# Batch 1's later K and Q rows in the tile buffers, its squares and scalings open to GpSimd, and a new set of priorities

## The chip, the cores and the metric

The kernel runs on one core of one Trainium2 chip. The metric is the device time of one execution in microseconds (us); smaller is better. A core has five engines with a queue each: TensorE (PE, with its weight loads as PEld), VectorE (DVE), ScalarE (ACT), GpSimd (POOL) and SyncE (SP). SP here issues DMAs only, and POOL issues DMAs beside its own arithmetic.

## What is computed

The reference, cut to what matters: cosine attention over 8 batches, 12 heads, 448 tokens and a head size of 64, then a Fourier mix over tokens and channels, a layer norm and a feed-forward part with 768 and 3072 channels.

```python
q_n = q / (np.linalg.norm(q, axis=-1, keepdims=True) + 1e-06)
k_n = k / (np.linalg.norm(k, axis=-1, keepdims=True) + 1e-06)
scores = np.matmul(q_n, k_n.transpose(0, 1, 3, 2)) / tau
attn = softmax(scores)                       # over the last axis
x = np.matmul(attn, v)                       # (8, 448, 768) after joining the heads
mixed = np.real(np.fft.fft(np.fft.fft(x, axis=1), axis=2))
u = x + mixed
un = (u - mean(u)) / np.sqrt(var(u) + 1e-06)
out = u + np.maximum(un @ w_ch1, 0.0) @ w_ch2
```

## The kernel before

The batches go through the same chain one after another, each overlapping its neighbours: load K and Q, normalise their rows, transpose them, multiply Q by K, exponentials, multiply by V, divide, Fourier mix, layer norm, the product with W1, the positive part, the product with W2, store. PE does all products. The feed-forward products (line 1864 with W1, line 2008 with W2) are most of its work; the attention of the following batch is laid between them.

**The order is planned, not written.** Every step is handed to a planner (class `Plan`) as an operation with the engines that may run it, an estimated duration for each, what it reads and writes, and a priority. `schedule` builds one queue for each engine: it takes, for the engine that can start earliest, the ready operation of best priority. Two tables have the last word. `SHIFT` adds a number of its own to the priority of each of 2833 operations. `HOME` pins an operation to one engine where the code would allow several; in the kernel before it has 70 entries. At run time each engine works through its queue strictly in order and waits on semaphores.

**Batches 0 and 1** are normalised by `first_norm` (line 1179), later ones by `norm` (line 1337). `first_norm` works in groups of head pairs: for batch 0 pair 0, pairs 1 and 2, pairs 3 to 5; for batch 1 pairs 0 to 2 and pairs 3 to 5. Each group has a K part, a Q part and a tail part (the last 64 tokens of both). For each part:

- a load from HBM, issued by SP (line 1231);
- a square into a scratch buffer (line 1249), on ACT for batch 1;
- a reduction over the 64 values of a head on DVE (line 1253);
- logarithm, exponential and reciprocal in `norms` (lines 1173 to 1177), once for a group;
- a scaling of each pair's rows, K and Q at line 1276, tails at line 1272, on DVE for batch 1 and on DVE or POOL for batch 0;
- PE transposes (lines 1299 to 1324) and copies out of PSUM (lines 1290 and 1334).

**Buffers.** Raw rows of batch 0 lie in TX, which later holds sums of W2. Raw rows of batch 1 lie in the place of W2 (W2b, chunks 10 to 23), and the squares of its first Q rows in W2b, chunks 7 to 9. So in `build` the loads of W2's later pieces wait for batch 1: two for the reduction of that square, the others for the scalings. W1's and W2's pieces are loaded by POOL's queue (lines 1154 and 1155), at most three under way. Batch 2's rows go to STG, three buffers in turn (line 1365), and their first load waits for an early piece of W2. E0 and E1 hold the exponentials (line 1442) of alternate head pairs.

**The filler.** `fill` puts small matmuls (line 2258) into gaps of PE's queue: up to the first feed-forward product, and from there to 20 us before the planned end.

Other lines that are named below: 1464, 1477 (Q by K), 1495, 1501 (by V), 1739 (the sum u), 1769 (the layer norm's square), 1797 (copy of transposed rows), 1959 (products with W1 in the last two batches), 1979 (what joins them), 2045 (DVE's addition to the output), 1387 and 2034 (POOL's scalings and additions of later batches), 1653 and 2207 (copies in the Fourier mix).

Of the kernel before, what the change touches and what calls it, by code (L numbers as in the profile page):

```python
# [973 lines left out]
class Kern:  # L974
# [204 lines left out]
    def first_norm(self, b):  # L1179
# [47 lines left out]
        for g, a, n, nt, R3, L, ps in parts:  # L1227
# [9 lines left out]
            for i, (nm, buf, names) in enumerate(ps):  # L1237
# [3 lines left out]
                for j0, j1 in ((0, m),) if b or g < 2 else [(j, j + 1) for j in range(m)] if i < 2 else ((0, m),):  # L1241
# [6 lines left out]
                    def square(e, sq=sq, y_=y_):  # L1248
                        return e.activation(sq, y_, ACTF.Square) if e is self.nc.scalar else e.tensor_tensor(sq, y_, y_, AluOp.mult)
# [1069 lines left out]
```

## Time and profile before

| what | value |
|---|---|
| median of three timed runs | 575.24 us (574.73 to 575.6) |
| the profiled execution, its own time | 575.0 us |
| its span, first to last instruction | 573.2 us |
| granted TensorE clock | 1.000 |
| DMA | 62.19 MB, mean 108 GB/s |
| MB read from HBM, written | 51.90, 11.01 |

A row of the profile names a source line, an engine, an operation and the buffers it writes and reads, then a count, busy microseconds and the mean length in ns. Behind the second bar stands the idle time of that engine just before these instructions, and what ended it ("<-DVE SM L1253" means that a DVE instruction of line 1253 that writes SM released it). A row of waits reads: who waited, for whom, microseconds in all, how often, the longest one. A row of the table by stages gives the stretch, its length, busy time and count for each engine, the granted clock and the DMA share and rate. A busy PE is not PE at its peak, because the lengths of matmuls overlap; PE's idle time is the firmer figure.

### The profile page before, as it was taken

To read this page: it belongs to the slowest core of one execution; us is meant where nothing else is said; L and a number is where in the kernel's file an instruction comes from. 1 tells how busy PE (TensorE), PEld (TensorE's weight loads), DVE (VectorE), ACT (ScalarE), POOL (GpSimd) and SP (SyncE) were. 2 spreads that over 40 slices of the span, in tenths; PEclk is the share of its full clock that TensorE was granted. 3 is DMA by queue.
4 is the path that set the end of the run, shared out by engine and by line. 5 is a ranking of instruction groups with operands and counts; after the bars stand their busy time and mean duration, and the time that the engine had idled before them with its cause. 6 is when DMAs were issued, how large, how long until landed. Compare 5 with 4: busy or idle time off the path is not lost.

```text
span 573.2 us, 16025 instructions
## 1 busy us (share of the span) xinstructions
PE 553.7 (97%) x6616; PEld 432.9 (76%) x6616; DVE 434.0 (76%) x923; ACT 392.9 (69%) x734; POOL 224.4 (39%) x332
## 2 busy tenths in 40 slices
PE   3899999999999899999999999999999999999998
PEld 2578887686787687878778688687886876959695
DVE  9889868987469867986789669965679379886353
ACT  7998976576776885578648886686665761948171
POOL 8522414356328542702380736443524003041304
PEclk9999999999999999999999999999999999999999
DMA  9999997976359645963496569461691200132001
GB/s 213 170 241 202 164 195 108 163 173 111 111 82 113 158 88 111 155 145 70 95 157 76 99 138 125 105 140 23 136 87 27 72 2 17 42 48 66 24 34 56
DMA packets 183945, 62.19 MB, mean 108 GB/s; under 512 B 166688, under 2 KB 181664, under 8 KB 183872
## 3 DMA queue, kind: packets, MB, share of 16 engines
q1 hardware_dynamic: 129824, 38.35, 35.2%
q0 software_dynamic: 54048, 22.81, 32.1%
q8 instruction: 52, 0.85, 0.6%
q14 instruction: 21, 0.17, 0.1%
HBM read 51.90 MB, written 11.01 MB: 110 GB/s over the span
## 4 chain that ended last, share of the span: by engine, by line
PE 78%; DVE 8%; ACT 6%; issue 3%; POOL 2%; DMA 2%; SPq 1%; POOLq 0%; DVEq 0%; ACTq 0%
PE PS L1864 28%; PE PS L2008 26%; PE PS L1959 7%; PE PS L1501 5%; PE PS L1464 5%; PE PS L1495 2%; PE PS L1477 1%; DMA TX<-in_q_dram 1%; ACT F L1769 1%; POOL QH L1387 1%; DVE F L1547 1%; POOL OUTB L2034 1%; PE PS L1685 1%; DVE OUTB L2045 1%; DVE X L1521 1%
## 5 line engine op out<-in xcount | busy, mean ns | idle before, releaser
L1864 PE MATMUL PS<-UNT,W1b 128*128 128x256 bf16 (+1 forms) x1728 | 185.4, 264 | 0.3 <-DVE UNT L1797 0.2
L1442 ACT ACTIVATE E<-PS 128x900 bf16<-128x900 f32 (+1 forms) x192 | 148.7, 827 | 30.3 <-PE PS L1464 24.3
L1864 PEld LDWEIGHTS PS<-UNT,W1b 128*128 128x128 bf16 x1728 | 153.4, 98 | 20.1 <-issue 1.9
L2008 PE MATMUL PS<-W2b,HQ 128*128 128x384 bf16 x720 | 124.9, 326 | 0.0
L1387 POOL TENSOR_TENSOR QH<-STG,SM 128x256 bf16<-128x256 f32 x126 | 84.4, 696 | 86.8 <-DVE SM L1177 65.0
L2008 PEld LDWEIGHTS PS<-W2b,HQ 128*128 128x128 bf16 x720 | 68.8, 98 | 43.1 <-issue 0.4
L2034 POOL TENSOR_TENSOR OUTB<-OUTB,U 128x192 f32<-128x192 f32 x72 | 51.6, 737 | 118.2 <-ACT OUTB L2029 115.6
L2008 PE MATMUL PS<-TX,HQ 128*128 128x384 bf16 (+2 forms) x444 | 76.4, 322 | 0.9 <-DVE OUTB L2045 0.5
L1880 ACT ACTIVATE HQ<-PS 128x512 bf16<-128x512 f32 x86 | 51.2, 595 | 28.8 <-PE PS L1864 27.6
L2108 DVE TENSOR_TENSOR HQ<-HQ 128x1536 bf16<-128x1536 bf16 (+1 forms) x73 | 54.1, 744 | 12.2 <-ACT HQ L1880 7.0
L2008 PEld LDWEIGHTS PS<-TX,HQ 128*128 128x128 bf16 x444 | 41.5, 98 | 27.9 <-DVE OUTB L2045 2.4
L1374 ACT ACTIVATE QH<-STG 128x384 f32<-128x384 f32 x84 | 43.1, 519 | 17.6 <-DVE SM L1376 11.6
L1376 DVE TENSOR_REDUCE SM<-QH 128x6 f32<-128x384 f32 x84 | 45.3, 544 | 11.3 <-ACT QH L1374 11.0
L1501 PE MATMUL PS<-VB,E 128*128 128x65 bf16 x1152 | 51.6, 193 | 0.0
L2067 POOL DMA_INDIRECT out_dram<-OUTB,IDX x21 | 23.7, 1127 | 69.2 <-DVE OUTB L2045 43.4
L1501 PEld LDWEIGHTS PS<-VB,E 128*128 128x128 bf16 x1152 | 47.8, 97 | 1.3
L1880 DVE TENSOR_SCALAR HQ<-PS 128x512 bf16<-128x512 f32 x40 | 27.4, 685 | 23.9 <-PE PS L1864 23.8
L1495 PE MATMUL PS<-VZ,E 128*128 128x130 bf16 x192 | 41.6, 219 | 2.0 <-issue 1.9
L1727 DVE SCALAR_TENSOR_TENSOR U<-ACG,X 128x768 bf16<-128x768 f32 (+4 forms) x39 | 39.5, 1023 | 0.9
L2029 ACT ACTIVATE OUTB<-PS 128x384 f32<-128x384 f32 x36 | 17.7, 491 | 32.2 <-PE PS L2008 29.4
L1464 PE MATMUL PS<-QK 64*128 64x225 bf16 (+2 forms) x864 | 39.2, 227 | 0.5 <-ACT QK L1290 0.5
L1464 PEld LDWEIGHTS PS<-QK 64*128 64x128 bf16 x864 | 25.6, 95 | 13.2 <-issue 6.6
(195 smaller groups left out, 784.5 us busy)
## 6 DMA issues: line engine op xcount, KB each, us to landing
STG<-in_q_dram SPq DMA_DIRECT2D x18, 384.0 KB, 3.9
STG<-in_k_dram SPq DMA_DIRECT2D x18, 384.0 KB, 3.9
VB<-in_v_dram POOLq DMA_DIRECT2D x24, 192.0 KB, 6.4
W2b<-in_moe_w_ch_dram POOLq DMA_DIRECT2D x12, 384.0 KB, 7.4
...
W2b<-in_k_dram SPq DMA_DIRECT2D x2, 576.0 KB, 9.1
W2b<-in_q_dram SPq DMA_DIRECT2D x2, 576.0 KB, 15.9
```

Source lines behind the costliest of these rows:

```text
L1374: P.add("act", lambda a, sq=sq, src=buf[:, w * x:w * x + w]: a.activation(sq, src, ACTF.Square), t_act(w), pr, f"sq{i}_{b}", reads=bn, wri ...
L1376: P.add("dve", lambda v, o=SS[:, i, H // ns * x:H // ns * (x + 1)], sq=sq: v.tensor_reduce(o, sq.rearrange("p (h d) -> p h d", d=DH), AX.X ...
L1387: r = v.tensor_tensor(v3(qh)[:, h:h + 4], v3(buf)[:, h:h + 4], RN[:, i, h:h + 4].unsqueeze(2).to_broadcast((128, 4, DH)), AluOp.mult)
L1442: return a.activation(o, self.PS[:, bk:bk + nc_, 0:SQ2], ACTF.Exp, scale=1.0 / self.tau)
L1464: i = pe.matmul(self.PS[:, bk + h, c0:c0 + n], self.KT[r, jj, kt * 128:(kt + 1) * 128], self.QT[r, jj, cols], start=True, stop=True)
L1495: r = pe.matmul(o, st(6), self.VZ[:, j, :], start=not split, stop=(split and i == 0), skip_group_check=True)
L1501: r = pe.matmul(o[:, 65 * h:65 * h + 65], st(2 * kt + h), self.VB[:, kt, 2 * j + h, :], start=(split and i == h == kt == 0), stop=((not sp ...
L1864: r = pe.matmul(self.PS[:, bk, x * n:(x + 1) * n], self.W1b[:, j, ft * 128:(ft + 1) * 128], self.UNT[:, j, cs], start=(j == 0), stop=(j == ...
L1880: return e.activation(o, i, ACTF.Relu) if e is self.nc.scalar else e.tensor_relu(o, i)
L2008: r = pe.matmul(self.PS[:, bk, 0:n], lhs(f), rhs(f), start=(start and f == 0), stop=(stop and f == NF // 2 - 1), skip_group_check=True)
L2034: r = g.tensor_tensor(self.OUTB[:, ob, xs], self.OUTB[:, ob, xs], self.U[:, ut, xs], AluOp.add)
L2108: P.add("dve", lambda v: v.tensor_tensor(cs(o), cs(a), cs(bq), op), 0.16 + 0.3 * len(ks), -0.5, f"{nm}{ks[0]}_{b}", reads=rd, writes=[x fo ...
```

## The change

In words:

- Batch 1's raw rows of the first group, and the K rows of the second, land in TX; the Q rows and tails of the second land in STG's second and third buffers. Their loads wait for the readers of batch 0's rows that lie there (`told`).
- The squares of batch 1's first Q rows go to E1 instead of W2b. W2's loads no longer wait for batch 1.
- Batch 2's loads into these two STG buffers wait for batch 1's rows in them.
- Squares and scalings of batch 1 may also run on POOL (as may batch 0's squares outside the first group), a square there in pieces of 192 columns.
- The second filler ends 12 us after the first feed-forward product.
- `SHIFT` has a new number for each of its 2833 operations. `HOME` has 206 entries. For the squares and scalings: all of batch 0 are pinned as they were or to ACT and DVE, the first of the K squares of pairs 3 to 5 newly to ACT; of batch 1 all are pinned (squares to ACT, scalings to DVE) but the square of the second K rows and four scalings (K of pair 1, tails of pairs 1, 2 and 5).

The diff without the two tables:

```diff
-PIECE = {"sinp": 1.1, r"sc[KQ]\d_0": 0.95, r"scT\d_0": 0.42, ...
+PIECE = {"sinp": 1.1, r"sc[KQ]\d_[01]": 0.95, r"sq[KQT]\d_[01]": 0.54, r"scT\d_[01]": 0.42, ...
...
-            hf = flat(self.W2b[:, 10:24, :]).bitcast(F32)
-            sw = flat(self.W2b[:, 7:10, :]).bitcast(F32)
+            hf = self.tf[:, 1536:9216].bitcast(F32)
+            sf = flat(self.STG[:])
+            sw = self.E[1][:, 0:2304].bitcast(F32)
...
-            sqn = [[o0, ["SQW"], ["OUT1b", "OUT1d"]], [o0, o0, ["OUT1b", "OUT1d"]]]
+            sqn = [[o0, ["SQW"] + [f"E1_{c}" for c in range(7)], ["OUT1b", "OUT1d"]], [o0, o0, ["OUT1b", "OUT1d"]]]
...
-            K, Q, R = [hf[:, o + x + y * ja:o + x + y * (ja + n)] for x, y in ((0, 384), (1152, 384), (2304, 128))]
+            K, Q, R = [(sf[:, DM + x - 1152 + y * ja:DM + x - 1152 + y * (ja + n)] if b and g and x else hf[:, o + x + y * ja:o + x + y * (ja + n)])
+                       for x, y in ((0, 384), (1152, 384), (2304, 128))]
...
+            told = {}
+            if b:
+                told = {"k": ["Sk1_0", "Sq0_0", "Sq1_0"], "q": ["Sq1_0", "St0_0", "Sk2_0"], "t": ["Sk2_0"]} if g == 0 else {"k": ["Sk2_0", "Sq2_0"]}
...
-                                        dma=(f"lh{g}{nm}{b}", 16 * len(dm)), serve=sv, after=gate, order=self.loads[-1:] if b == 0 else ()))
+                                        dma=(f"lh{g}{nm}{b}", 16 * len(dm)), serve=sv, after=gate + [r for x in told.get(nm, ()) for r in P.rd[x]], order=self.loads[-1:] if b == 0 else ()))
...
-                    es = ("act",) if b else (("act", "dve"), ("act", "dve"), ("act", "dve", "pool"))[g]
+                    es = ("act", "dve") if b == g == 0 else ("act", "dve", "pool")
...
-                        return e.activation(sq, y_, ACTF.Square) if e is self.nc.scalar else e.tensor_tensor(sq, y_, y_, AluOp.mult)
+                        if e is self.nc.scalar:
+                            return e.activation(sq, y_, ACTF.Square)
+                        k = 192 if e is self.nc.gpsimd else w
+                        for x in range(0, w, k):
+                            xs = slice(x, min(x + k, w))
+                            r = e.tensor_tensor(sq[:, xs], y_[:, xs], y_[:, xs], AluOp.mult)
+                        return r
...
-                    sc.append(P.add("dve" if b else ("dve", "pool"), fn, ...
+                    sc.append(P.add(("dve", "pool"), fn, ...
...
-                ... f"ld_{kind}{t}_{b}", writes=bn,
+                ... f"ld_{kind}{t}_{b}", writes=bn + ({1: ["Sq1_1"], 2: ["Sq1_1", "St1_1"]}.get(s, []) if b == 2 else []),
...
-                for c in (3, 4):
-                    self.w[12 + c].deps.add(self.sqw)
-                for c in range(5, 12):
-                    self.w[12 + c].deps.update(self.raw1[3] + (self.raw1[4] if c > 7 else []))
...
-        self.P.fill(first, self.est - 20.0, self.id_op, warm(self.W1b[:, 0, 0:128]), 0.75)
+        self.P.fill(first, first + 12.0, self.id_op, warm(self.W1b[:, 0, 0:128]), 0.75)
```

`sums`, which later overwrites TX with sums of W2, waits in addition for batch 1's rows in TX.

More of the change, by code (lines that the diff above doesn't have):

```diff
@@ L82 @@
 SHIFT = {
-    "iota": {0: -4743.9411}, "iotak": {0: -3749.0012}, "cst": {0: 2295.738}, "iotad": {0: 1504.4864}, "rown": {0: 3564.9514},
-    "tqd": {0: 5876.6502, 1: 5614.4443}, "trd": {0: 5875.7288}, "tpd": {0: -1558.5233, 1: 550.4848}, "tad": {0: 4737.392},
-    "tqs": {0: 4545.6213, 1: 5636.9779}, "trs": {0: 4448.6198}, "tps": {0: -162.6304, 1: -1607.3824}, "tas": {0: -178.9521}, "ktd0": {0: 1975.3204},
[4 rows of a table removed]
-    "mask": {0: 35657.0228}, "sinp": {0: 48649.0823}, "half": {0: 440.6683, 1: 3500.6271}, "sinn": {0: 17464.9799}, "ldt": {0: 44319.0778},
[510 rows of a table removed]
+    "iota": {0: 1055.999}, "iotak": {0: 412.7235}, "cst": {0: 2977.9783}, "iotad": {0: 3978.0742}, "rown": {0: 1060.8053},
@@ L601 @@
+    "tqd": {0: 3803.646, 1: -2997.4266}, "trd": {0: 2432.3949}, "tpd": {0: -2992.3091, 1: -8184.413}, "tad": {0: 15630.733},
+    "tqs": {0: -3148.9211, 1: -3159.9506}, "trs": {0: -2641.2921}, "tps": {0: -3159.405, 1: -3160.3855}, "tas": {0: 5801.7804}, "ktd0": {0: 1123.7336},
[4 rows of a table added]
+    "mask": {0: 44111.9307}, "sinp": {0: 59268.5429}, "half": {0: 3949.4502, 1: 10817.8207}, "sinn": {0: 56970.1711}, "ldt": {0: 45259.1831},
[507 rows of a table added]
 }
 HOME = {
-    "tqd": {0: "dve", 1: "dve"}, "trd": {0: "dve"}, "tas": {0: "act"}, "sinp": {0: "dve"}, "half": {0: "pool", 1: "act"}, "sqK0_0": {0: "act"},
@@ L613 @@
-    "ek1_1": {0: "act"}, "ek2_1": {0: "dve"}, "eq2_1": {0: "act"}, "relu0_0": {0: "act"}, "relu4_0": {0: "act"}, "relu8_0": {0: "dve"},
-    "relu12_0": {0: "act"}, "relu16_0": {0: "act"}
+    "tqd": {0: "dve", 1: "dve"}, "trd": {0: "dve"}, "tad": {0: "act"}, "tas": {0: "act"}, "sinp": {0: "dve"}, "half": {0: "pool", 1: "act"},
+    "sqK0_0": {0: "act"}, "sqQ0_0": {0: "act"}, "sqT0_0": {0: "dve"}, "scK0_0": {0: "dve"}, "scQ0_0": {0: "dve"}, "scT0_0": {0: "dve"},
+    "ek0_0": {0: "act"}, "eq0_0": {0: "act"}, "et0_0": {0: "dve", 1: "act"}, "sqK1_0": {0: "dve"}, "sqQ1_0": {0: "act"}, "scK1_0": {0: "dve"},
@@ new lines @@
+    "scQ1_0": {0: "dve"}, "scT1_0": {0: "dve"}, "scK2_0": {0: "dve"}, "scQ2_0": {0: "dve"}, "scT2_0": {0: "dve"}, "ek1_0": {0: "dve"},
+    "eq1_0": {0: "act"}, "eq2_0": {0: "act"}, "et1_0": {0: "dve", 1: "act"}, "sqK2_0": {0: "act", 1: "act", 2: "dve"},
+    "sqQ2_0": {0: "act", 1: "act", 2: "act"}, "sqT2_0": {0: "act"}, "scK3_0": {0: "dve"}, "scQ3_0": {0: "pool"}, "scT3_0": {0: "dve"},
+    "scK4_0": {0: "pool"}, "scQ4_0": {0: "dve"}, "scT4_0": {0: "dve"}, "scK5_0": {0: "pool"}, "scQ5_0": {0: "pool"}, "scT5_0": {0: "pool"},
@@ new lines @@
+    "ek3_0": {0: "dve"}, "eq3_0": {0: "act"}, "eq4_0": {0: "dve"}, "ek5_0": {0: "act"}, "eq5_0": {0: "dve"}, "et2_0": {0: "dve", 1: "dve"},
+    "gc2_0": {0: "dve"}, "cd0": {0: "dve"}, "cd1": {0: "act"}, "cd2": {0: "dve"}, "cd3": {0: "act"}, "cd4": {0: "act"}, "cd5": {0: "dve"},
+    "halfd": {0: "act"}, "eu00_0": {0: "act"}, "eu01_0": {0: "dve"}, "eu10_0": {0: "dve"}, "eu11_0": {0: "dve"}, "eu20_0": {0: "act"},
[5 rows of a table added]
+    "gc1_1": {0: "act"}, "te0_1": {0: "dve"}, "relu0_0": {0: "act"}, "relu4_0": {0: "act", 1: "dve"}, "relu8_0": {0: "dve"}, "relu12_0": {0: "act"},
@@ new lines @@
+    "relu16_0": {0: "act"}, "relu20_0": {0: "dve", 1: "dve"}, "relu2_0": {0: "dve"}, "relu10_0": {0: "dve"}, "relu18_0": {0: "dve"},
+    "relu22_0": {0: "dve"}, "te1_2": {0: "act"}, "relu16_1": {0: "act", 1: "dve"}, "relu6_1": {0: "act"}, "relu18_1": {0: "act", 1: "dve"},
+    "relu20_1": {0: "act"}, "relu2_1": {1: "dve"}, "relu14_1": {1: "dve"}, "ct0": {0: "dve"}, "ct2": {0: "dve"}, "ct3": {0: "dve"},
+    "te1_3": {0: "act"}, "relu2_2": {0: "act"}, "relu16_2": {0: "dve", 1: "act"}, "relu6_2": {0: "dve"}, "relu8_2": {0: "dve", 1: "act"},
@@ new lines @@
+    "relu22_2": {0: "dve"}, "relu0_2": {1: "act"}, "relu12_2": {1: "act"}, "relu4_2": {1: "act"}, "ktd4": {1: "act"}, "gc1_4": {0: "act"},
+    "z_4": {0: "act"}, "relu2_3": {0: "act"}, "relu14_3": {0: "act", 1: "act"}, "relu16_3": {0: "dve"}, "relu6_3": {0: "act", 1: "act"},
+    "relu18_3": {0: "dve"}, "relu22_3": {0: "act"}, "relu0_3": {1: "act"}, "relu12_3": {1: "dve"}, "relu4_3": {1: "act"}, "relu8_3": {1: "act"},
+    "relu20_3": {1: "act"}, "relu10_3": {1: "act"}, "ktd5": {0: "dve", 1: "dve"}, "gc1_5": {0: "act"}, "z_5": {0: "act"}, "te0_5": {0: "act"},
@@ new lines @@
+    "relu0_4": {0: "act"}, "relu2_4": {0: "act"}, "relu16_4": {0: "act"}, "relu6_4": {0: "act"}, "relu18_4": {0: "act"}, "relu20_4": {0: "act"},
+    "relu22_4": {0: "dve"}, "te0_6": {0: "act"}, "te1_6": {0: "act"}, "relu0_5": {0: "act"}, "relu14_5": {0: "act", 1: "act"},
+    "relu18_5": {0: "act", 1: "act"}, "relu8_5": {0: "dve"}, "relu22_5": {0: "dve", 1: "act"}, "relu12_5": {1: "act"}, "te0_7": {0: "act"},
+    "relu2_6": {0: "dve"}, "relu14_6": {0: "act"}, "relu6_6": {0: "dve"}, "relu8_6": {0: "act"}, "relu20_6": {0: "dve"}, "relu22_6": {0: "act"},
@@ L615 @@
+    "c1r1_6": {0: "dve", 1: "dve"}, "c2r1_6": {0: "act", 2: "dve", 3: "act"}, "c3r1_6": {0: "dve", 1: "act"},
+    "c41_6": {0: "dve", 1: "act", 2: "act", 3: "act"}, "c1r0_7": {0: "dve", 2: "act"}, "c2r0_7": {0: "act", 2: "act"},
+    "c3r0_7": {0: "dve", 1: "dve", 2: "act"}, "c40_7": {1: "dve"}, "c1r2_7": {1: "dve", 2: "dve"}, "c2r2_7": {1: "act"},
+    "c3r2_7": {0: "dve", 1: "dve"}, "c42_7": {1: "act"}
 }
 LATE = {r"W[12]w?_\d+": 1.5, "tmd": 2.0, r"sq\d_\d": 1.5, r"sq[KQT]\d_1": 1.5, r"ktd\d": 2.0, r"qdup\d": 2.0, r"qk\d._[2-7]": 1.5, r"pv\d\d_[2-7]": 1.5, r"pv\d\d_1": 1.0, r"h\d+_[1-7]": 0.5}
-PIECE = {"sinp": 1.1, r"sc[KQ]\d_0": 0.95, r"scT\d_0": 0.42, r"sc\d_\d": 0.6, r"f[avm]\dp_\d": 0.54, r"t\d\d": 0.94}
+PIECE = {"sinp": 1.1, r"sc[KQ]\d_[01]": 0.95, r"sq[KQT]\d_[01]": 0.54, r"scT\d_[01]": 0.42, r"sc\d_\d": 0.6, r"f[avm]\dp_\d": 0.54, r"t\d\d": 0.94}
@@ L1215, in first_norm @@
             o, ja = 2688 * (a // 3), a % 3
-            K, Q, R = [hf[:, o + x + y * ja:o + x + y * (ja + n)] for x, y in ((0, 384), (1152, 384), (2304, 128))]
+            K, Q, R = [(sf[:, DM + x - 1152 + y * ja:DM + x - 1152 + y * (ja + n)] if b and g and x else hf[:, o + x + y * ja:o + x + y * (ja + n)])
+                       for x, y in ((0, 384), (1152, 384), (2304, 128))]
             nt = (3, 0, 3)[g] if b == 0 else n
-            R3 = hf[:, o + 2304 + 128 * ja:o + 2304 + 128 * (ja + nt)]
+            R3 = R if b else hf[:, o + 2304 + 128 * ja:o + 2304 + 128 * (ja + nt)]
             L = [("k", [(heads(K, n), self.heads(self.k, b, 2 * a, 2 * n, 0, 3, 128, 192))], 0.64 * n),
@@ L1244, in first_norm, with square @@
                     y_ = y[:, wd[i] * j0:wd[i] * j1]
-                    es = ("act",) if b else (("act", "dve"), ("act", "dve"), ("act", "dve", "pool"))[g]
+                    es = ("act", "dve") if b == g == 0 else ("act", "dve", "pool")
                     sn = sqn[g][i] if j0 == 0 else [f"{sqn[g][i][0]}_{j0}"]
-                    def square(e, sq=sq, y_=y_):
-                        return e.activation(sq, y_, ACTF.Square) if e is self.nc.scalar else e.tensor_tensor(sq, y_, y_, AluOp.mult)
-                    P.add(es, square, [{"act": t_act(w), "dve": t_dve(w), "pool": 0.1 + 0.0023 * w}[e] for e in es], pg[g], f"sq{nm}{g}_{b}",
+                    def square(e, sq=sq, y_=y_, w=w):
+                        if e is self.nc.scalar:
[5 more added lines that the diff above has]
+                        return r
+                    P.add(es, square, [{"act": t_act(w), "dve": t_dve(w), "pool": 0.1 * -(-w // 192) + 0.0023 * w}[e] for e in es], pg[g], f"sq{nm}{g}_{b}",
                           reads=names, writes=sn, order=[self.exps[-1]] if b else [])
@@ L1279, in fn @@
                                                .to_broadcast((128, 3, 2, DH)), AluOp.mult)
-                    sc.append(P.add("dve" if b else ("dve", "pool"), fn, ((t_dve(378), 0.95) if i < 2 else (0.3, 0.55)) if b == 0 else t_dve(378) if i < 2 else 0.3, pg[g] + 0.1 * j, f"sc{nm}{jj}_{b}", reads=names + [rn[i][j]],
+                    sc.append(P.add(("dve", "pool"), fn, (t_dve(378), 0.95) if i < 2 else (0.3, 0.55), pg[g] + 0.1 * j, f"sc{nm}{jj}_{b}", reads=names + [rn[i][j]],
                                     writes=qhn[g][i] if j == 0 else [qhn[g][i][-1] + f"_{j}"],
@@ L1365, in fn @@
                         sy.dma_start(dst, src).then_inc(sem, 16)
-                self.loads.append(P.add("sp", fn, 0.36 * len(dm), pr, f"ld_{kind}{t}_{b}", writes=bn,
+                self.loads.append(P.add("sp", fn, 0.36 * len(dm), pr, f"ld_{kind}{t}_{b}", writes=bn + ({1: ["Sq1_1"], 2: ["Sq1_1", "St1_1"]}.get(s, []) if b == 2 else []),
                                         dma=(key, 16 * len(dm)), after=gate, serve=1.75))
@@ L2185, in sums @@
         X = lambda x, k: self.TX[:, x, 4 * k:4 * k + 4, :]
-        old = ["ID", "rowf", "CSp", "QLt", "QLu", "QLu_1", "QLv", "QLv_1", "QLv_2", "QM", "QMt"] + [f"S{x}{g}_0" for x in "kqt" for g in range(3)] + [
+        old = ["ID", "rowf", "CSp", "QLt", "QLu", "QLu_1", "QLv", "QLv_1", "QLv_2", "QM", "QMt"] + [f"S{x}{g}_0" for x in "kqt" for g in range(3)] + ["Sk0_1", "Sq0_1", "St0_1", "Sk1_1"] + [
             f"QM{t}_{j}" for t in ("", "t") for j in (1, 2)]
```

8 lines of the change are left out of this document (removed), and 1030 rows, old and new, of tables (HOME, SHIFT).

## The prediction

> **What bounds the kernel now.** I read the page first, then the busy time of each engine stage by stage, then the matrix engine's waits. The page has the shares:
>
> ```profile
> span 573.2 us, 16025 instructions
> PE 553.7 (97%) x6616; PEld 432.9 (76%) x6616; DVE 434.0 (76%) x923; ACT 392.9 (69%) x734; POOL 224.4 (39%) x332
> ```
>
> PE leads, but a share over the whole span hides where it stands still. The table by stages (stretch; its length; busy us and instructions of PE, PEld, DVE, ACT, POOL; granted clock; DMA) shows that:
>
> ```profile
> 0.00:12.00 12.00, 3.93 (x31) 2.82 (x32) 10.74 (x25) 8.61 (x14) 9.66 (x34) 1.00 0.83 229
> 12.00:48.00 36.00, 32.05 (x482) 24.36 (x482) 30.94 (x81) 33.84 (x55) 13.47 (x20) 1.00 1.43 202
> 48.00:60.00 12.00, 10.90 (x172) 9.95 (x173) 11.74 (x38) 10.34 (x28) 6.05 (x8) 1.00 1.42 184
> 60.00:180.00 120.00, 120.00 (x1291) 92.99 (x1292) 92.32 (x190) 85.69 (x161) 50.14 (x69) 1.00 0.92 138
> 180.00:200.00 20.00, 18.24 (x170) 12.49 (x168) 17.97 (x40) 14.59 (x33) 12.77 (x16) 1.00 0.69 132
> 200.00:470.00 270.00, 269.86 (x3323) 213.12 (x3322) 200.33 (x421) 188.74 (x348) 105.67 (x150) 1.00 0.65 99
> 470.00:516.00 46.00, 44.08 (x491) 32.96 (x489) 42.38 (x83) 24.37 (x54) 13.34 (x15) 1.00 0.15 34
> ```
>
> Four things are to be seen. From 60 to 180 PE is never idle. After that it loses 1.76 us (180 to 200), 0.14 (200 to 470) and 1.92 (470 to 516): 3.8 us in all. From 48 to 60, where the first feed-forward products run, it loses 1.1 us, and some of its busy time is filler. Before 48 ACT is busy for 33.84 of 36 us: there batch 0's own chain sets the pace, and PE waits for it. The clock is at 1.00 in every stage. So time can be won only in three places: the chain before 48, the stage to 60, and the 3.8 us afterwards.
>
> The filler (the matmuls of line 2258) by stages, PE and PEld:
>
> ```profile
> 48.00:60.00 12.00, 1.34 (x18) 1.02 (x18) 1.00 1.42 184
> 60.00:570.00 510.00, 0.00 (x0) 0.00 (x0) 1.00 0.61 97
> ```
>
> So 48 to 60 holds 1.1 + 1.34 = 2.4 us without useful work. What PE waited for, first in 48 to 60, then after 60:
>
> ```profile
> PE PS L2258 <- DVE CS L2207: 0.4, 1, 0.4
> PE PS L1324 <- ACT QK L1290: 0.3, 1, 0.3
> PE PS L1864 <- DVE UNT L1797: 0.2, 1, 0.2
> PE PS L1311 <- DVE TX L1272: 0.2, 1, 0.2
> ```
>
> ```profile
> PE PS L1495 <- issue: 1.5, 1, 1.5
> PE PS L1959 <- DVE HQ L1979: 0.8, 1, 0.8
> PE PS L1959 <- DMA UNT<-F: 0.5, 1, 0.5
> PE PS L2008 <- DVE OUTB L2045: 0.5, 1, 0.5
> PE PS L2008 <- ACT E L1653: 0.2, 1, 0.2
> ```
>
> Of the waits after 60, 1.5 us (0.8 + 0.5 + 0.2) are for work that stood in a queue of DVE or ACT. Those an order of priorities can move. The 1.5 us "issue" and the 0.5 us of a DMA it reaches less surely.
>
> **The change, part by part.** The profiled execution took 575.0 us, 1.8 us more than its span. The median of the three timed runs is 575.24, so 0.2 us are added at the end. About 0.2% (1.15 us) is what a measurement can tell from no change.
>
> *Staging.* Batch 1's K and Q rows no longer land in W2's place but in the buffer TX and in STG. TX still holds batch 0's rows, so three loads of batch 1 now wait until those are read. The first K load waits for batch 0's first three head pairs only. The first Q load, the first tail loads and the second K load wait for the scalings of batch 0's last three pairs. The second Q load and its tails go to STG and wait for nothing new. Today:
>
> ```profile
> 22.37 0.37 SPq L1231 DMA_DIRECT2D W2b<-in_k_dram  x1
> 22.78 0.59 SPq L1231 DMA_DIRECT2D W2b<-in_q_dram  x1
> ...
> 32.41 5.61 SPq L1231 DMA_DIRECT2D W2b<-in_k_dram  x1
> ```
>
> ```profile
> 28.64 0.86 POOL L1276 TENSOR_TENSOR QH<-TX,SM 128x384 bf16<-128x384 f32 x1
> ```
>
> ```profile
> W2b<-in_q_dram SPq DMA_DIRECT2D x2, 576.0 KB, 15.9
> ```
>
> ```profile
> 48.38 1.15 ACT L1249 ACTIVATE W2b<-W2b 128x1152 f32<-128x1152 f32 x1
> ```
>
> The last of these scalings, on POOL, ends at 28.64 + 0.86 = 29.5. The first Q load issued at 22.78 would go at 29.5, 6.7 us later. With its 15.9 us to landing it is there at 45.4. The square that reads it (the one into W2b) starts at 48.38, so 3.0 us of cover remain. Behind the waiting load on SP's queue stand batch 1's other loads, which SP issues until 32.41 + 5.61 = 38.0 anyway. I take 0. The cost lies between nothing and the late-rows rival below. A gain would have to come through W1, whose pieces share the DMA engines with fewer loads until 29.5; but no wait of PE in 48 to 60 is for a DMA, so I count none.
>
> *The square's scratch* moves from W2's place to E1. It must wait for batch 0's last products from E1, and batch 1's exponentials into E1 wait for the reduction of that square:
>
> ```profile
> 49.93 1.34 DVE L1253 TENSOR_REDUCE SM<-W2b 128x18 f32<-128x1152 f32 x1
> ```
>
> ```profile
> 60.84 1.73 ACT L1442 ACTIVATE E<-PS 128x900 bf16<-128x900 f32 x2
> ```
>
> The reduction ends at 51.3, and batch 1's first exponential starts at 60.84: 0, with 9.5 us of cover. If rows came late, this cover would go first.
>
> *W2's loads* lose their wait for batch 1's reductions and scalings. Their last issue now, and the first product with W2:
>
> ```profile
> 79.86 0.70 POOL L1155 DMA_DIRECT2D W2b<-in_moe_w_ch_dram  x1 [2.22 <-DMA W2b<-in_moe_w_ch_dram]
> ```
>
> ```profile
> 90.82 0.33 PE L2008 MATMUL PS<-W2b,TX 128*128 128x384 bf16 x1
> ```
>
> PE has other work without a gap from 60 to 90.82, so an earlier W2 gains nothing by itself: 0. Batch 2's loads, which wait for an early part of W2, may also go sooner; batch 1's rows in STG then hold two of their three buffers. Also 0.
>
> *Squares and scalings on GpSimd.* The table HOME has the last word on the engine. In the changed table every square of batch 0 is pinned to ACT or DVE, and of batch 1's six squares five are pinned to ACT; only the second K square is free. Of batch 1's eighteen scalings four are free: one K and three tails. So at most this moves:
>
> ```profile
> L1249 ACT ACTIVATE OUTB<-W2b 128x1152 f32<-128x1152 f32 x3 | 3.5, 1164 | 0.7 <-DVE SM L1253 0.7
> ```
>
> ```profile
> 55.28 1.03 DVE L1276 TENSOR_TENSOR TX<-W2b,SM 128x384 bf16<-128x384 f32 x2
> 56.23 0.49 DVE L1272 TENSOR_TENSOR TX<-W2b,SM 128x128 bf16<-128x128 f32 x2
> ```
>
> That is 1.16 us off ACT, and 1.03/2 + 3 x 0.49/2 = 1.25 us off DVE. DVE is the fuller one from 48 to 60 (11.74 of 12), and three of PE's four waits there are for it. So I count the 1.25 us as PE time, against 2.4 us lost there, and ACT's 1.16 at nothing. The bounds are 0 (all four stay on DVE) and -2.4. What POOL costs DVE is below: two scalings of DVE beside two of POOL.
>
> ```profile
> 23.55 2.30 DVE L1276 TENSOR_TENSOR QH<-TX,SM 128x384 bf16<-128x384 f32 x2
> ```
>
> ```profile
> 23.39 2.04 POOL L1276 TENSOR_TENSOR QH<-TX,SM 128x384 bf16<-128x384 f32 x2 [3.97 <-DVE SM L1177]
> ```
>
> They took 2.30 us instead of 1.03, so 0.64 us more for each. The Trainium skill's page "SBUF — State Buffer" (section "Who interferes with whom") says that a DVE instruction with two SBUF inputs and a GpSimd instruction that reads SBUF exclude each other, and that the second to issue blocks fully until the first is done. By it the -1.25 us would turn into a loss whenever the six pieces of the square meet DVE's scalings; the trace agrees that they hold each other up (0.64 us each), and the rival below has the price in rows of this case.
>
> *One square of batch 0* (the first of the last three K squares) is pinned to ACT, where batch 0's chain is:
>
> ```profile
> 10.88 0.52 ACT L1249 ACTIVATE W2b<-TX 128x384 f32<-128x384 f32 x1
> ```
>
> Up to +0.5, and nothing where ACT has one of its few gaps; with ACT at 33.84 of 36 us I take +0.4.
>
> *The priorities.* Every number of SHIFT is new, and HOME pins 206 instructions instead of 70. What order comes out can't be read off the diff. The bounds are the lost times: of the 3.8 us after 60, all or none, or new gaps as long as these. I take the 1.5 us that are waits in a queue of DVE or ACT. *The filler after the first product* now ends 12 us after it instead of 20 us before the end. Past 60 there is none today, so 0.
>
> Sum: 575.0 - 1.25 - 1.5 + 0.4 = 572.65, and with the 0.2 us to the median 572.8.
>
> **The rivals.**
>
> *All gaps closed, faster still.* The new order closes the 2.4 us before 60 and the 3.8 us after it: 575.24 - 6.2 = 569.0. If it also shortens the chain before 48, where PE has 3.95 idle us and filler besides, it is below that. For it: nearly all waits are for DVE or ACT, and POOL is free for 22 of 36 us. Against: ACT is full there, and hardly anything of batch 0 changes engine.
>
> *No change.* The gaps move instead of closing, because another transfer or chain comes last a microsecond later: 575.2. For it: PE is 97% busy, and every batch has a chain of its own that must end before PE runs dry.
>
> *Batch 1's rows come late, slower.* The longest landing among today's loads of line 1231 in 20 to 40 is in the row below (shortest, median, longest).
>
> ```profile
> DMA to landing us min/median/max: 7.5/11.8/19.5
> ```
>
> The point from which it decides is a landing after 48.4. A load that goes at 29.5 and takes 19.5 lands at 49.0, 0.6 late; one that takes the last place in SP's queue (32.41 today) and 19.5 us lands at 51.9, 3.5 late. PE has little else between the first token tile's products and batch 1's, so it loses what is late; the middle, 2.1 us, gives 577.3. Against it: the STG loads can go first, and then SP's queue is through no later than now.
>
> *POOL's pieces hold up DVE, slower.* Six pieces of 192 columns, each near the length of the nearest row:
>
> ```profile
> L2034 POOL TENSOR_TENSOR OUTB<-OUTB,U 128x192 f32<-128x192 f32 x72 | 51.6, 737 | 118.2 <-ACT OUTB L2029 115.6 <-DVE RD L1519 1.2
> ```
>
> If half of them meet a two-input instruction of DVE in 48 to 60 and hold it 0.74 us, PE loses 2.2 us: 577.4. It decides only if they are put there, and before 48 POOL has room for them.
>
> **How the numbers follow.** Forecast 0.43, all gaps closed 0.14, no change 0.21, late rows 0.14, POOL's pieces 0.08. So faster 0.57, same 0.21, slower 0.22. The forecast's own range is 571 to 574. The whole range goes from 568.0, a little below the all-closed case, to 577.5 at the slower rivals.
>
> **What would show it.** Right: 180 to 200 and 470 to 516 each with under 1 us of PE idle; 48 to 60 with less filler; the first product of line 1864 still near 48; the square of the first Q rows not waiting for a DMA. Wrong: ACT's squares of batch 1 released by "DMA TX<-in_q_dram" (late rows); DVE's scalings above 0.55 us in 48 to 60 (pieces); a first feed-forward product moved by over a microsecond either way, since I give the chain before 48 only +0.4; new gaps of PE after 60, where there is no filler any more.

## The result, and the profile after

The changed kernel takes 578.35 us (median of 5 runs, 578.22 to 578.89); the kernel before, run beside it, 575.6 us. The ratio is 1.0054, with a 95% interval of 1.0039 to 1.0069: slower by about 3 us, where 2.4 us less was forecast. The profiled execution took 578.32 us. Its page and its table by stages (stretch; length; busy us of PE, PEld, DVE, ACT, POOL; granted clock; DMA):

```profile
span 576.3 us, 16005 instructions
PE 555.3 (96%) x6604; PEld 435.0 (75%) x6604; DVE 438.2 (76%) x940; ACT 382.1 (66%) x717; POOL 221.4 (38%) x332
```

```profile
12.00:48.00 36.00, 32.00 (x444) 24.16 (x442) 29.06 (x79) 32.57 (x52) 13.23 (x20) 1.00 1.64 202
48.00:60.00 12.00, 10.19 (x166) 9.35 (x163) 10.12 (x35) 8.89 (x23) 6.41 (x8) 1.00 1.31 190
60.00:180.00 120.00, 118.97 (x1298) 92.12 (x1296) 96.96 (x200) 80.74 (x154) 44.95 (x63) 1.00 0.89 133
180.00:200.00 20.00, 18.59 (x162) 12.38 (x161) 19.64 (x44) 15.16 (x34) 13.38 (x17) 1.00 1.18 120
200.00:470.00 270.00, 269.60 (x3318) 213.98 (x3316) 197.50 (x420) 188.44 (x354) 107.16 (x154) 1.00 0.66 102
470.00:516.00 46.00, 44.47 (x505) 33.44 (x503) 43.29 (x86) 24.16 (x50) 12.11 (x13) 1.00 0.09 27
```

From 48 to 60 PE now stands idle for 1.81 us instead of 1.10, and from 60 to 180 for 1.03 us instead of none. Between 180 and 516 it loses 3.34 us instead of 3.82. ACT and DVE have less to do from 12 to 48 than before (32.57 and 29.06, not 33.84 and 30.94): work has been pushed out of that stage. What it was is in the single rows. First the start of the chain on ACT, of before and of after. Line 1173 (after: 1191) is the logarithm of a group's norms, line 1442 (1471) the exponentials, the ACT_TABLE_LOAD follows their end:

```profile
9.47 0.31 ACT L1173 ACTIVATE SM<-SM,MV 128x14 f32<-128x14 f32 x1
...
15.80 2.98 ACT L1442 ACTIVATE E<-PS 128x900 bf16<-128x900 f32 x4
...
37.37 1.28 ACT L1131 ACT_TABLE_LOAD   x1
```

```profile
10.88 0.94 ACT L1273 ACTIVATE W2b<-TX 128x384 f32<-128x384 f32 x2 [0.55 <-DMA TX<-in_k_dram]
11.73 0.50 ACT L1191 ACTIVATE SM<-SM,MV 128x14 f32<-128x14 f32 x2
...
17.55 1.73 ACT L1471 ACTIVATE E<-PS 128x900 bf16<-128x900 f32 x2 [0.28 <-PE PS L1493]
...
39.09 1.28 ACT L1149 ACT_TABLE_LOAD   x1
```

The first group's logarithm has gone from 9.47 to 11.73, together with the second group's and behind two squares that wait for a DMA. Everything up to the end of the exponentials is 1.7 us later. Then the later stage: ACT's squares of batch 1 (line 1273), the first product with W1 (line 1893, 48.17 before), and the load of batch 1's first Q rows, as issued and in the chain of waits:

```profile
47.05 1.16 ACT L1273 ACTIVATE OUTB<-TX 128x1152 f32<-128x1152 f32 x1 [0.85 <-DMA TX<-in_k_dram]
...
52.83 1.16 ACT L1273 ACTIVATE E<-TX 128x1152 f32<-128x1152 f32 x1 [1.51 <-DMA TX<-in_q_dram]
```

```profile
51.53 1.17 PE L1893 MATMUL PS<-UNT,W1b 128*128 128x128 bf16 x18 [0.27 <-DVE UNT L1826]
```

```profile
32.89 19.92 DMA TX<-in_q_dram
52.81 0.02 issue
52.83 1.17 ACT E L1273
54.00 0.02 issue
54.02 1.36 DVE SM L1282
```

So there are two suspects. The first product comes 3.36 us later (the order). And ACT stands still for 1.51 us until the first Q rows land at 52.81 (the rows); batch 1's first transposes move from 56.66 to 60.69.

### The profile page after: what moved, and what is told of

It is laid out like the page before. It is cut to its first block, busy times and chain, and to the rows that moved or that the text cites. A ratio compares the mean times of both kernels' runs of the same rounds, so it can differ in the third digit from the quotient of the medians.

```text
span 576.3 us, 16005 instructions
## 1 busy us (share of the span) xinstructions
PE 555.3 (96%) x6604; PEld 435.0 (75%) x6604; DVE 438.2 (76%) x940; ACT 382.1 (66%) x717; POOL 221.4 (38%) x332
## 4 chain that ended last, share of the span: by engine, by line
PE 84%; DVE 8%; DMA 5%; ACT 1%; issue 1%; SPq 1%; DVEq 0%
PE PS L2037 30%; PE PS L1893 28%; PE PS L1988 7%; PE PS L1493 6%; PE PS L1530 5%; DMA TX<-in_q_dram 3%; PE PS L1524 2%; PE PS L1506 2%; DMA TX<-in_k_dram 1%; DVE HQ L2137 1%; PE PS L1340 1%; PE PS L1714 1%; SPq L1254 1%; DVE U L1756 1%; PE PS L1657 1%
## 5 line engine op out<-in xcount | busy, mean ns | idle before, releaser
L1471 ACT ACTIVATE E<-PS 128x900 bf16<-128x900 f32 (+1 forms) x192 | 149.3, 828 | 35.1 <-PE PS L1493 29.5
L1416 POOL TENSOR_TENSOR QH<-STG,SM 128x256 bf16<-128x256 f32 x126 | 83.2, 686 | 87.6 <-DVE SM L1195 81.0
L2037 PEld LDWEIGHTS PS<-W2b,HQ 128*128 128x128 bf16 x720 | 68.8, 98 | 45.4 <-issue 2.0
L2063 POOL TENSOR_TENSOR OUTB<-OUTB,U 128x192 f32<-128x192 f32 x72 | 49.8, 712 | 111.9 <-ACT OUTB L2058 110.8
L1909 ACT ACTIVATE HQ<-PS 128x512 bf16<-128x512 f32 x79 | 47.1, 596 | 34.2 <-PE PS L1893 33.5
L1909 DVE TENSOR_SCALAR HQ<-PS 128x512 bf16<-128x512 f32 x47 | 32.3, 688 | 27.6 <-PE PS L1893 27.4
L1448 POOL DMA_DIRECT2D VB<-in_v_dram x24 | 25.5, 1071 | 28.2 <-PE PS L1530 21.5
```

The lines of the kernel that those rows point to most:

```text
L1416: r = v.tensor_tensor(v3(qh)[:, h:h + 4], v3(buf)[:, h:h + 4], RN[:, i, h:h + 4].unsqueeze(2).to_broadcast((128, 4, DH)), AluOp.mult)
L1471: return a.activation(o, self.PS[:, bk:bk + nc_, 0:SQ2], ACTF.Exp, scale=1.0 / self.tau)
L1909: return e.activation(o, i, ACTF.Relu) if e is self.nc.scalar else e.tensor_relu(o, i)
L2037: r = pe.matmul(self.PS[:, bk, 0:n], lhs(f), rhs(f), start=(start and f == 0), stop=(stop and f == NF // 2 - 1), skip_group_check=True)
L2063: r = g.tensor_tensor(self.OUTB[:, ob, xs], self.OUTB[:, ob, xs], self.U[:, ut, xs], AluOp.add)
```

## The experiments

The planner reacts to every edit with another order, so each experiment takes the choice away from it. The five queues are written out as lists, and the planner may only place the next operation of each list:

```diff
+QUEUES = {"pe": """...""", "act": """...""", "dve": """...""", "pool": """...""", "sp": """..."""}
...
                 for op in ready[e]:
+                    if op.name + f".{op.nth}" != self.pin[e][len(self.order[e])]:
+                        continue
```

The lists are those planned in the kernel before ("old order") or in the changed kernel ("new order"), with the moves named below. In the diffs k0, q0, t0 are batch 1's first K, Q and tail rows, k1, q1, t1 the second. The lists stand ahead of the code, so line numbers differ: the squares are line 1448, 1424, 1425 or 1426 there, the logarithm 1348 or 1366, the exponentials 1617 or 1646, the products with W1 2068. Nothing of the computation is left out in any of them. All ratios are to the kernel before on the same chip; the first product with W1 and the wait of q0's square for its rows are from the profiled execution, in us:

| run | rows | order | ratio (95%) | first product | wait of q0's square |
|---|---|---|---|---|---|
| before | W2's place | old | 1 | 48.17 | 0 |
| after | TX, q0 last | new | 1.0054 (1.0039 to 1.0069) | 51.53 | 1.51 |
| e1 | TX, q0 last | old | 1.0051 (1.0036 to 1.0065) | 48.35 | 3.12 |
| e2 | W2's place | new | 1.0044 (1.0030 to 1.0058) | 50.77 | 0 |
| e3 | TX, q0 ahead of k1 | new | 1.0061 (1.0046 to 1.0075) | 51.06 | 0 |
| e4 | TX, q0 last | old to 40 us, then new | 1.0065 (1.0052 to 1.0079) | 50.69 | 2.18 |
| e5 | q0 in STG | old | 1.0002 (0.9993 to 1.0010) | 48.06 | 0 |
| e6 | W2's place, q0 made late | old | 1.0064 (1.0047 to 1.0081) | 48.53 | 3.30 |
| e9 | q0 in STG | new | 1.0044 (1.0032 to 1.0057) | 50.78 | 0 |
| e10 | q0 in STG | old to 40 us, then new | 1.0012 (1.0003 to 1.0020) | 49.48 | 0 |

**The two parts apart (e1 to e4).** e1 and e2 make one part each, e3 and e4 mend one each:

```diff
 e1: code of after, old order, but
-SP: k0 t0 k1 q1 q0 t1
+SP: t1 q1 k0 t0 k1 q0
 e2: code of before, new order, but SP: k0 t0 k1 q1 q0 t1
 e3: code of after, new order, but
-SP: t1 q1 k0 t0 k1 q0
+SP: t1 q1 k0 t0 q0 k1
-ACT: ... square of k1, square of q0, relus ... first copies of batch 1
+ACT: ... square of q0, relus ... square of k1, first copies of batch 1
 e4: code and SP of after; on the other engines the old order
     for what starts before 40 us there, then the new order
```

> The changed kernel's staging (TX and STG, its SP order for batch 1's six loads), but the queues of PE, ACT, DVE and POOL in the order of the kernel before. Order theory (the loss is batch 0's chain, put in a worse order, and the late Q rows hide behind it): the first product of the feed-forward net is within 0.7 us of 48.2 and the time is 575.6, within 0.8. Late-rows theory (the loss is the wait for batch 1's first Q rows, which land at about 52.8): ACT reaches the Q0 square near 48.4, waits some 4 us for the DMA, and the time is 578.0 or more. If both cost something alone and hide in one another: 577.0 to 577.6.

> The kernel before with its rows staged in W2's place and its SP order of batch 1's six loads, but the queues of PE, ACT, DVE and POOL in the order of the changed kernel. Order theory: the first product of the feed-forward net stays near 51.5, the time is 578.3, within 0.8. Late-rows theory: the rows land in time, the 1 us that the changed kernel wins between 470 and 516 is kept, and the time is 574.6, within 0.8. If each costs something alone: 577.5.

> The changed kernel with two moves: batch 1's first Q load goes ahead of its second K load on SP, and ACT's square of the second K rows goes behind the relus, just ahead of batch 1's first copies out of PSUM. Late-rows theory: ACT's wait of 1.5 us for the first Q rows and of 0.9 us for the second K rows goes, batch 1's first transposes come 2 to 3 us sooner (60.7 to about 58), and the time is 576.0 or less. Order theory: the first product stays at 51.5 and the time stays within 0.8 of 578.35.

> The changed kernel, its staging and its loads, but what the kernel before starts in its first 40 us (batch 0's chain and the tables) is queued on each engine as there; the rest in the changed kernel's order. Order theory: the first product comes back from 51.5 to about 48.2 and the time falls by 2.5 to 3.5 us, to 575.4, within 0.8. Late-rows theory: the Q rows still land near 52.8, ACT waits longer for them (4 us instead of 1.5), and the time stays at 578, within 0.8.

Measured: 578.25, 577.9, 579.35 and 579.58 us, against 575.86 for the kernel before. Neither theory alone stands: e1 is slow although its first product is in time, and e2 is slow although no square waits for its rows. The third case is right, each costs something alone and they hide in one another; only its 577.0 to 577.6 was too low. e3 and e4, which were to mend one fault each, win nothing: they came out 0.2 and 0.8 us above the highest that was expected of them. In e3 the moved square stands just ahead of batch 1's copies, at 58.98; that is not followed further. In e4's profiled run the first product was late all the same (50.69). One part of that is a first exponential at 16.63, after a wait of ACT for the third K load; the larger part is in the order after 40 us, as e10 shows below. What late rows do in e1, on ACT and then on PE (by the microsecond: busy us and instructions, granted clock, DMA):

```profile
51.85 1.16 ACT L1448 ACTIVATE E<-TX 128x1152 f32<-128x1152 f32 x1 [3.12 <-DMA TX<-in_q_dram]
```

```profile
53.73 4.47 PE L2068 MATMUL PS<-UNT,W1b 128*128 128x128 bf16 x48 [2.53 <-ACT TX L2084]
```

```profile
52.00:53.00 1.00, 0.00 (x0) 1.00 1.20 208
53.00:54.00 1.00, 0.27 (x5) 1.00 1.17 203
54.00:55.00 1.00, 1.00 (x15) 0.55 1.15 208
55.00:56.00 1.00, 1.00 (x12) 0.50 0.93 167
56.00:57.00 1.00, 1.00 (x12) 0.50 0.50 85
57.00:58.00 1.00, 1.00 (x17) 0.75 1.47 102
```

The relu that PE waits for (line 2084) stands behind the waiting square on ACT. PE loses 2.53 us, and then another (0.45 + 0.5 + 0.5 + 0.25) = 1.7 us because the clock is granted at about half for three microseconds. At the end 2.9 us remain of these 4.2: the kernel before loses 1.10 us from 48 to 60 as well, and from 180 to 516 e1 happens to stand idle 1.0 us less than it. In the changed kernel the order delays ACT so far that the square waits for 1.51 us only, PE's gaps are short and the clock stays at 1.00. That is how the two hide in one another.

**Is it the late rows, or something else of the staging (e5, e6)?** e5 keeps the staging but swaps its halves, so that the rows wanted first lie in STG, which is free. e6 keeps the old staging and makes only q0 late:

```diff
 e5: code of after, old order
-                told = {"k": ["Sk1_0", "Sq0_0", "Sq1_0"], "q": ["Sq1_0", "St0_0", "Sk2_0"], "t": ["Sk2_0"]} if g == 0 else {"k": ["Sk2_0", "Sq2_0"]}
+                told = {"k": ["Sk1_0", "Sq0_0", "Sq1_0"]} if g == 0 else {"k": ["Sk2_0", "Sq2_0"], "q": ["Sq1_0", "St0_0", "Sk2_0"], "t": ["Sk2_0"]}
...
     (K, Q, R: q0, t0 in STG and q1, t1 in TX; the names in sums and in batch 2's loads follow)
+SP: t0 q0 k0 k1 q1 t1
 e6: code of before, old order
+                if (b, g, nm) == (1, 0, "q"):
+                    self.loads[-1].deps.update(P.rd["Sk2_0"])
-SP: k0 t0 k1 q1 q0 t1
+SP: k0 t0 k1 q1 t1 q0
```

> The staging with its two sets of rows swapped: batch 1's first Q rows and tails (wanted near 48 us) land in STG, which is free from the start, and the second ones (wanted after 60) land in TX and wait for batch 0. SP's order: first tails, first Q, first K, second K, second Q, second tails. All other queues in the order of the kernel before. Late-rows theory: ACT's square of the first Q rows no longer waits for a DMA, batch 1's first transposes are back near 56.7, and the time is that of the kernel before, 575.8, within 0.8. Rival (the staging costs by something else: the square's scratch in E1, the W2 loads that go without a wait, the traffic): 577.3 or more, although no square waits for its rows.

> The kernel before, rows in W2's place, its own order, with one edit: batch 1's first Q load goes last on SP and waits for the scalings of batch 0's last three K pieces, as in the changed kernel. Late-rows theory: the rows land near 52, ACT's square waits about 3 us for them, and this alone gives the 578.2 of the staging-only run, within 0.8. Rival (something else of the staging): 575.8 to 576.6.

Measured: 575.46 and 579.36 us, against 575.52. The square of q0 in e5 and in e6:

```profile
48.22 1.15 ACT L1448 ACTIVATE E<-STG 128x1152 f32<-128x1152 f32 x1
```

```profile
52.09 1.16 ACT L1426 ACTIVATE W2b<-W2b 128x1152 f32<-128x1152 f32 x1 [3.30 <-DMA W2b<-in_q_dram]
```

With q0 early the whole staging (scratch in E1, W2's loads without a wait, the traffic) costs nothing that can be measured. With q0 late, and nothing else changed, the kernel loses 2.7 to 4.7 us. The cause of the staging's loss is settled.

**Where in the order (e7, e8, e13, e14)?** All four have the code of before and the old order, with one piece of the new one:

```diff
 e7: what the new order starts before 12 us is queued as there
 e8: ACT: the square of k0 ahead of the second sines
 e13: ACT at the start
-tas sqK0 sqQ0 sins tad ldt0 half ln0 nrm0 sqQ1 ...
+tas sins ldt0 sqK0 sqQ0 half tad ln0 nrm0 sqQ1 ...
 e14: ACT at the start
-tas sqK0 sqQ0 sins tad ldt0 half ln0 nrm0 sqQ1 sqK2b sinn ...
+tas sqK0 sqQ0 sins tad ldt0 half sqQ1 sqK2a sqK2b ln0 ln1 nrm0 nrm1 sinn ...
```

Here sqK0, sqQ0, sqQ1 and sqK2a, b are batch 0's squares by group (sqK2a was on DVE before), ln and nrm the logarithm and exponential of a group, sins, sinn and ldt0 the sines and the table load; DVE's sums follow.

> The kernel before with one part of the new order: what the changed kernel starts in its first 12 us (the tables and the norms of batch 0's first two groups, the second group's logarithm and exponential together with the first's) is queued as there, the rest as before. If the order's loss lies in the first norms: the first exponential comes 1.7 us later (17.5), the first product too (49.9), and the time is 577.3, within 0.8. If it lies in the place of batch 1's K square: 575.8, within 0.6.

> The kernel before with one other part of the new order: ACT's square of batch 1's first K rows goes right behind the table load, ahead of the second sines and their table load, as in the changed kernel. If the order's loss lies here: the copies out of the transform and the first product come 1.1 us later (49.3) and the time is 577.0, within 0.8. If it lies in the first norms: 575.8, within 0.6, as the square stands ahead of the transform's copies in both orders and only the sines move.

> The kernel before with one half of the front: ACT's first sines and the table load go ahead of the squares of batch 0's first K and Q rows (which then start at 7.3 instead of 4.25), and DVE's sums follow; the logarithm and exponential of the first group stay by themselves. If the front's loss comes from the late squares: first exponential near 17.5, 577.5 or more. If it comes from joining the two groups' norms: the first logarithm still goes when the squares are summed, near 9.5 to 9.8, the first exponential near 15.8, and the time is 575.5, within 0.6.

> The kernel before with the other half of the front: the squares of the first rows stay ahead of the sines, but the first group's logarithm and exponential wait for the second group's sums, as in the changed kernel. If the loss comes from joining the norms: first logarithm near 11.7, first exponential near 17.5, first product near 50, and 578.2, within 0.8. If it comes from the late squares: 575.5, within 0.6.

Measured: e7 578.39 us, ratio 1.0060 (1.0046 to 1.0074); e8 575.61, 1.0006 (0.9997 to 1.0015); e13 576.39, 1.0007 (0.9997 to 1.0017); e14 578.54, 1.0043 (1.0030 to 1.0057). ACT in e13 and in e14:

```profile
10.38 0.29 ACT L1348 ACTIVATE SM<-SM,MV 128x14 f32<-128x14 f32 x1
...
16.19 2.98 ACT L1617 ACTIVATE E<-PS 128x900 bf16<-128x900 f32 x4
```

```profile
11.29 0.94 ACT L1424 ACTIVATE W2b<-TX 128x384 f32<-128x384 f32 x2 [0.96 <-DMA TX<-in_k_dram]
12.13 0.50 ACT L1348 ACTIVATE SM<-SM,MV 128x14 f32<-128x14 f32 x2
...
17.84 2.54 ACT L1617 ACTIVATE E<-PS 128x900 bf16<-128x900 f32 x3 [0.46 <-PE PS L1639]
```

The loss at the start is in joining the norms. In e14 the first group's logarithm stands behind two squares of batch 0's last K rows, which wait for the third K load; the first exponential moves from 15.80 to 17.84, the first product to 50.30, and the end by 2.5 us. The joined logarithm stands at the head of batch 0's chain, and everything up to the first product moves with it. The late squares (e13, its logarithm at 10.38 instead of the expected 9.5 to 9.8) and the place of k0's square (e8) cost nothing that their intervals tell from none, and at most 1.0 us. e7 and e14 also have the new order in POOL's first operations and in a few table steps of DVE; these were not tried apart.

**Both mended (e9, e10).** The swap of e5 with the new order, then with the old order up to 40 us:

```diff
 e9: code and SP of e5, new order
 e10: code and SP of e5; old order for what starts before 40 us there, then the new order
```

> The changed kernel with only its staging swapped as in the swap run (batch 1's first Q rows and tails in STG, loaded first) and PE, ACT, DVE and POOL in the changed kernel's order. If the two losses hide in one another, mending the rows alone leaves what the order alone costs: 577.9, within 0.8, first product near 51, no wait of a square for its rows. If the rows are the only loss that counts at the end: 575.6.

> As the run above, and besides what the kernel before starts in its first 40 us is queued as there; only what comes after 40 us stands in the changed kernel's order. If all of the order's loss lies before 40 us and the rest is worth nothing: 575.5, within 0.6. If the changed kernel's smaller loss between 470 and 516 (1.5 us idle instead of 1.9, and 1 us won back) comes from its order: 574.5. If the order after 40 us costs too: 576.5 or more.

Measured: 578.39 and 576.17 us, against 575.23. e9 keeps the order's whole loss, and e10 keeps 0.7 us of it (0.2 to 1.2), so something after 40 us costs too. It lies between the end of the exponentials (the ACT_TABLE_LOAD) and the first product: 10.8 to 10.9 us in before, e5, e6, e7, e8, e13 and e14 (e1: 11.2), but 12.3 to 12.4 us in all runs with the new order after 40 us (after, e2, e3, e4, e9, e10). DVE in e5 and in e10, with the sums u of a token tile (line 1943) and the mean of the first tile (line 1969):

```profile
45.52 0.56 DVE L1943 SCALAR_TENSOR_TENSOR U<-PS,X 128x384 bf16<-128x384 f32 x1
...
46.12 0.21 DVE L1969 TENSOR_SCALAR MV<-ACG 128x1 f32<-128x1 f32 x1
```

```profile
45.48 0.55 DVE L1943 SCALAR_TENSOR_TENSOR U<-PS,X 64x384 bf16<-64x384 f32 x1
...
47.09 0.54 DVE L1943 SCALAR_TENSOR_TENSOR U<-PS,X 64x384 bf16<-64x384 f32 x1
...
47.56 0.20 DVE L1969 TENSOR_SCALAR MV<-ACG 128x1 f32<-128x1 f32 x1
```

In e5 DVE does the first tile's two sums and then its mean. In the new order three sums of other tiles and a copy stand ahead of the mean, which comes 1.44 us later, and the first product with it. No run moves these sums alone.

Nor does the new order show a saving later. PE from 180 to 516 in e1 (old order) and in e9 (new order):

```profile
180.00:200.00 20.00, 18.70 (x166) 1.00 1.09 133
200.00:470.00 270.00, 269.92 (x3321) 1.00 0.65 100
470.00:516.00 46.00, 44.61 (x503) 1.00 0.12 28
```

```profile
180.00:200.00 20.00, 18.37 (x166) 1.00 0.95 141
200.00:470.00 270.00, 268.68 (x3308) 1.00 0.67 99
470.00:516.00 46.00, 43.95 (x497) 1.00 0.09 27
```

Idle time there is 1.30 + 0.08 + 1.39 = 2.8 us in e1 and 5.0 us in e9, 3.8 in before, 3.3 in after. These are single executions, and the other runs lie between: 3.2 to 4.3 us with the old order (e5 to e8, e11 to e15), 3.1 us with the new one in e2. So the 0.5 us that the changed kernel seems to save late are within what runs of one order differ by; that the priorities save anything there is not shown.

**A shorter chain on purpose (e11, e15), and a square on POOL (e12).** All with the code, SP and old order of e5:

```diff
 e11: ACT: the last table load behind the transform's second copy, not ahead;
      square of k1 behind the norms of batch 1's first group; DVE: sum of t0 behind the first residual sums
 e15: as e11, the sum of t0 behind DVE's copy of the first normalised tile
 e12: ACT: without the square of k0; POOL: that square, in six pieces, ahead of W1's last load
```

> The swap run with batch 0's chain made shorter on purpose: ACT's last table load goes behind the second copy of the transform instead of ahead of it (the copy starts at 42.6 instead of 43.4), the square of batch 1's second K rows goes behind the norms of its first group, and DVE's sum of the tails behind the first residual sums. If the time follows the first product about one to one, as the front run says: first product 47.4 instead of 48.06 and 574.8, within 0.6. If another wait takes its place in 48 to 60: 575.5 or more.

> The short-chain run with DVE's sum of batch 1's tails moved once more, behind its copy of the first normalised tile: there it held that copy up by 0.4 us. If the time follows the first product: from the end of the exponentials to the first product 10.2 us instead of 10.65 (10.8 in the kernel before), 574.6, within 0.5, below the kernel before. If what was won there is lost in 48 to 60: 575.3, within 0.4.

> The swap run with the square of batch 1's first K rows on GpSimd, in six pieces of 192 columns, ahead of the last load of W1 on that queue; ACT is rid of 1.15 us ahead of the transform's copy. If the pieces pass unhindered (4.4 us from about 37): the first product comes up to 0.9 us sooner and the time is 574.8, within 0.6. If they and the two-input instructions of DVE hold each other up, as the prediction's rival has it: DVE's additions at 38 to 42 take over 0.6 us each, its sum of the squares comes later than 41.3, and the time is 576.5 or more.

Measured: e11 574.9 us, 0.9992 (0.9983 to 1.0000); e15 575.29, 0.9996 (0.9986 to 1.0006); e12 576.73, 1.0020 (1.0011 to 1.0029). In e15 the chain is as short as expected: from the end of the exponentials (37.03) to the first product (47.27) it takes 10.24 us, 10.8 in before. e11 has 10.65 there as expected, but in its profiled run the exponentials end 1.3 us later than in before and the first product is at 49.32, not 47.4. The time does not follow the shorter chain; 0.56 us won there can't be told from nothing at the end. No version is shown to beat the kernel before. In e12, POOL, DVE and PE, and DVE's same additions in e5:

```profile
34.47 3.37 POOL L1453 TENSOR_TENSOR OUTB<-TX 128x192 f32<-128x192 f32 x6 [3.84 <-DMA TX<-in_k_dram]
...
36.86 1.26 DVE L1752 TENSOR_TENSOR F<-ACG 128x512 bf16<-128x512 bf16 x2
```

```profile
39.77 3.85 PE L2461 MATMUL PS<-TX 128*128 128x128 bf16 x66
43.46 0.36 PE L1837 MATMUL PS<-CS,ACG 128*65 128x225 bf16 x2
```

```profile
37.23 0.76 DVE L1751 TENSOR_TENSOR F<-ACG 128x512 bf16<-128x512 bf16 x2
```

A piece takes 0.56 us, and DVE's two additions take 1.26 us beside it instead of 0.76. That agrees with the rule of the Trainium skill's page "SBUF — State Buffer" (section "Who interferes with whom") that the two exclude each other, with less lost than a whole piece for each. But the 2 us on the way to the next product (43.46 instead of 41.36 in e5) are the kernel's own filler: the planner put 66 small matmuls there, and DVE's last input for that product is ready at 41.26. So e12 has the time that was expected of the rival, but mostly for another reason; it tells the price for DVE, not that of the square on POOL.

## Why the prediction was wrong

**Staging, taken as 0: wrong, 2.9 (e1) to 3.7 us (e6) alone.** This is the first step that failed: "The first Q load issued at 22.78 would go at 29.5, 6.7 us later. With its 15.9 us to landing it is there at 45.4." The row at 22.78 is another load. The answers on single DMA issues show it, both of before:

```profile
W2b<-in_q_dram SPq DMA_DIRECT2D x1, 96.0 KB, 7.5
```

```profile
26.61 4.29 SPq L1231 DMA_DIRECT2D W2b<-in_q_dram  x2
```

The one at 22.78 moves 96 KB, a tail. The two 576 KB loads of Q rows share the row at 26.61, and the single records of the trace put the first group's, the second of them, at 29.39. So 29.5 was no delay at all; the delay came from its place in the queue. The 15.9 us to landing were wrong too: they are the median of these two, which take, in order,

```profile
W2b<-in_q_dram SPq DMA_DIRECT2D x1, 576.0 KB, 14.3
```

```profile
W2b<-in_q_dram SPq DMA_DIRECT2D x1, 576.0 KB, 17.4
```

So already in the kernel before the rows land at 46.8, later than the 45.4 that was forecast for the kernel after, and the cover ahead of the square at 48.38 is 1.6 us, not 3.0. After the change the load is SP's last, at 32.89 (3.5 us later), and it needs 19.92 us instead of 17.4 (2.5 more). Landing at 52.81, 6.0 us later, it uses up the cover and more. The rival "rows come late" had the mechanism, the last place in SP's queue included, and a landing at 51.9. Its price of 2.1 us was the middle between 0.6 and 3.5 us late; in e1 the square waits 3.12 us, and the way to PE goes over the relus behind it and PE's clock. Against this rival stood that SP's queue would be through no later than now. That came true (last issue at 32.89, before 32.41), but the rows wanted first had become the last in it.

**The square's scratch in E1 and W2's loads without a wait, 0 each: right** (e5: 1.0002).

**Work to POOL, -1.25: nothing there.** In the new order not one of the free squares and scalings of batch 1 went to POOL; it has 332 instructions in both kernels. HOME said where work could go, and the sum took it as gone. The rival "POOL's pieces" could not happen for the same reason.

**A square of batch 0 pinned to ACT, +0.4: the right place, a sixth of the size.** It is one of the two squares in front of the joined logarithms (e14). The 0.52 us that it lasts matter little; that the two stand ahead of the first norms, and wait there for a DMA (0.96 us in e14), costs 2.5 us.

**Priorities, -1.5: the second step that failed.** It looked only at the queue waits after 60 and left the chain before 48, which the prediction itself named as one of three places where time can be won, without a bound for loss. The order lost 2.5 us there (e2, e9), at the joined norms (e14) and at the sums ahead of the first tile's mean (e10, 0.7 us alone). That it saved something later is not shown (5.0 us idle from 180 to 516 in e9, 3.1 in e2, 3.8 in before). The test given in advance, "a first feed-forward product moved by over a microsecond", was the right one: 48.17 to 51.53. **The filler, 0:** no run here changes it alone.

**The sum.** The two losses, about 2.5 us (e2) and 2.9 us (e1), overlap to 3.1 us in the changed kernel: ratio 1.0054.
